# Moving sixteen subtractions to GpSimd and nine evictions to VectorE in a fused attention, MoE and MLP kernel

## The chip, the cores and the metric

The kernel runs on 1 core of one Trainium2 chip. The metric is the device time of one execution in microseconds (us). A core has a matrix engine (TensorE, PE in the profile, with its weight loads as PEld), a vector engine (VectorE, DVE), a scalar engine (ScalarE, ACT), GpSimd (POOL) and SyncE (SP), which here issues the transfers. Each engine works through its own instructions in the order in which they were issued, and waits where one needs a result that isn't there yet.

## What is computed

The reference has three stages, one after the other:

```
attn = softmax(mask(q @ k.T / 8)) @ v           # 4 batches, 8 heads, 576 positions, head size 64
x = soft mixture of experts(attn)               # 2304 tokens x 512, 8 experts of 4 slots
h = x @ w_in                                    # 2304 x 2048
g = where(h > 0, h, exp(min(h, 0)) - 1)
out = g @ w_out                                 # 2304 x 512
```

`w_in` (512 x 2048) and `w_out` (2048 x 512) arrive as 64-bit floats, the rest as 32-bit floats.

## The kernel before

The attention and the mixture of experts take the first 144 us and are issued in the order in which the code stands. The change lies in the last stage, the MLP, which is planned: the code builds a list of nodes (engine, estimated duration, what it depends on, a key that says by when it is wanted, the function that issues it), lays them out in time with a list scheduler (lines 1062 to 1102), and issues them in that order. For each engine the scheduler looks at the nodes that can start within 0.1 us of the earliest one and takes the one with the smallest key. Among the engines it takes the node that starts first. So the order on each engine is fixed before the kernel runs, from estimates, and at run time an engine can't pass over an instruction that waits.

The hidden size is cut into 16 blocks `f` of 128, the tokens into five groups (four of 512, one of 256). One unit of work is one group with one block. `SEGS` fixes the order of the units; the first ones use f = 0 and 1 for all groups. A unit is:

- `f_h` (line 974, PE): the hidden block into PSUM, from `M4` (`pers` in the trace), which is `w_in` times the mixture's 32 slot outputs;
- `f_e`, `f_r`, `f_g` (lines 978, 981 on ACT, 984 on DVE): the activation into the tile `g`. Line 984 reads PSUM and one SBUF tile;
- `f_hi` (line 990, ACT) and `f_lo` (line 994, DVE): `g` split into a rounded high part and the rest. Line 994 reads two SBUF tiles. The trace names the outputs `ghi`, `glo` or `rings`;
- `f_o` (lines 1016 to 1018, PE): for each 128 tokens three matmuls of 512 columns, high by high, high by low, low by high, added up in one of six PSUM banks (`ops`).

The weights have to be turned from 64-bit to 32-bit floats first. For each block of 128 x 512 this is line 727 (`dec_abs`) on ACT and lines 731, 735 and 741 (`dec_1` to `dec_3`) on DVE, where 735 and 741 read two SBUF tiles. For `w_out`, `out_nodes` then splits the block: line 928 on ACT writes the high part (`wh` or `w` in the trace), line 931 on DVE subtracts it from the decoded block (`wl` or `w`). This subtraction reads two SBUF tiles and runs once for each of the 16 blocks. All blocks of `w_in` pass the same decoding and then `m_nodes`, which makes `M4` with two matmuls (lines 883 and 894), two ACT instructions and line 900 on DVE.

A sum over f is done in several segments. The first segment of a token block is evicted from PSUM to SBUF (`part`) by ACT, line 1046, 18 of them; later ones are added to `part` by DVE (line 1048), the last is added and sent out (line 1051). `s` numbers the 128-token blocks in a group. An eviction's key is set by the moment at which the sixth product after it wants the same PSUM bank.

Ahead of the planned time `FT` the free time on PE is filled with matmuls whose result nobody uses (line 1111, `wps`): 0.9 of each planned gap.

Of the kernel before, what the change touches and what calls it, by code (L numbers as in the profile page):

```python
# [12 lines left out]
AF = mybir.ActivationFunctionType  # L13
# [6 lines left out]
def attn_moe_mlp(ctx, tc, q, k, v_l, v_s, phi, w1, w2, w_in, w_out, out):  # L20
    nc = tc.nc
    B, S, D = 4, q.shape[1] * q.shape[3] // 4, 64
# [32 lines left out]
    ]  # L55
    TB, SL, LD, LM, EPS = 24.7, 4.7, 2.7, -1.2, 0.1
    WP, HP = 256, 2
    K1, K2 = 0.0, 0.0
    FT, FW, M0 = 7.5, 0.9, ((0, 128), (128, 128), (256, 256))

    const = ctx.enter_context(tc.tile_pool(name="const", bufs=1))
# [290 lines left out]
    with tc.manual_schedule():  # L352
# [7 lines left out]
        for b in range(B):  # L360
            sm_ = smask[32 * b:32 * b + 32, 0, :]
            nc.gpsimd.affine_select(
                out=sm_, in_=sm_, compare_op=ALU.is_ge, fill=NEG, base=0,
# [3 lines left out]
        for e in range(2):  # L367
            nc.vector.memset(qk_t[2][1][:, e, 0:576], 0.0)
        nc.vector.tensor_copy(
            out=smask16.rearrange("p (a b) -> p a b", b=MR), in_=smask.to_broadcast([128, 16, MR])  # L370
# [14 lines left out]
        for b in range(B):  # L385
            lm = lmask[32 * b:32 * b + 32]
            nc.gpsimd.affine_select(
                out=lm[:, 0:32], in_=lm[:, 0:32], compare_op=ALU.is_ge, fill=NEG, base=0,
# [3 lines left out]
                out=lm[:, 32:64], in_=lm[:, 32:64], compare_op=ALU.is_ge, fill=NEG, base=-1,  # L392
# [29 lines left out]
        for x in (576, 1152):  # L422
            for e in range(2):
                w = x // 576 * 576
                nc.scalar.activation(
                    out=qk_t[2][1][:, e, x:x + w], in_=zero.to_broadcast([128, w]), func=AF.Copy,
                )
        for b in range(B):
            nc.scalar.activation(
                out=e0[32 * b:32 * b + 32].rearrange("p (g x) -> p g x", x=32),  # L430
                in_=ident[0:32, 0:32].unsqueeze(1).to_broadcast([32, B, 32]), func=AF.Copy,
# [146 lines left out]
        for f in emit_N(nu - 1):  # L578
# [41 lines left out]
            out=acc_sb[0], in0=acc1, scalar=wt[:, 1:2], in1=acc_sb[0], op0=ALU.mult, op1=ALU.add  # L620
# [14 lines left out]
        for x in (slice(0, 256), slice(256, 512)):  # L635
            nc.vector.scalar_tensor_tensor(
                out=acc_sb[1][:, x], in0=acc2[:, x], scalar=wt[:, 2:3], in1=acc_sb[0][:, x], op0=ALU.mult, op1=ALU.add
# [180 lines left out]
        NF = DFF // 128  # L818
# [18 lines left out]
        def node(eng, dur, deps, key, fn, alloc=None, at=0.0):  # L837
            nodes.append((eng, dur, list(deps), key, fn, alloc, at))
            return len(nodes) - 1
# [6 lines left out]
        due, need_h, need_w, now = [], {}, {}, TB  # L846
# [7 lines left out]
        d3, m_done, w_done = {}, {}, {}  # L854

        def decode_nodes(kind, i, c, key, rel, h0=0):
            at = loads.get((1 - kind, i, c), loads.get((1 - kind, i), 0.0))
            deps = [] if at else [dma[1 - kind, i]]
            k, z, h = ("ow"[kind], i, c), (512 - h0) / 512, slice(h0, 512)

            def f_abs():
                if not h0:
                    cnt["dec"] += 1
                    dec_of[k] = dec[:, cnt["dec"] % 8]
                dec_abs(w64[1 - kind, i][:, c, h], dec_of[k][:, h])

            def step(f):
                return lambda: f(w64[1 - kind, i][:, c, h], dec_of[k][:, h])

            n = node("A", 0.05 + 0.47 * z, deps, key - 3.0, f_abs, None if h0 else ("dec", rel), at)  # L870
            n = node("V", 0.065 + 0.27 * z, [n], key - 2.0, step(dec_1))
            n = node("V", 0.07 + 0.53 * z, [n], key - 1.4, step(dec_2))
            n = node("V", 0.07 + 0.53 * z, [n], key - 0.7, step(dec_3))
            d3[1 - kind, i, c, h0] = n
            return n
# [42 lines left out]
        def w_tile(d, s, f):  # L918
            if f // 8 not in d:
                d[f // 8] = slot(s, f"w{f}")  # L920
            return d[f // 8][:, 512 * (f % 8):512 * (f % 8) + 512]

        def out_nodes(f):
            key, rel = need_w[f] - 1.5 - LD, []
            x = decode_nodes(0, f // 4, f % 4, key, rel)

            def f_hi():
                nc.scalar.activation(out=w_tile(wo_hi, 0, f).bitcast(F32R), in_=dec_of["o", f // 4, f % 4], func=AF.Copy)

            def f_lo():  # L930
                nc.vector.tensor_tensor(
                    out=w_tile(wo_lo, 5, f).bitcast(F32R), in0=dec_of["o", f // 4, f % 4], in1=w_tile(wo_hi, 0, f),
                    op=ALU.subtract,
                )

            x = node("A", 0.52, [x] + ([d3[0, 1, c, 0] for c in range(4)] if f == 8 else []), key, f_hi)
            x = node("V", 0.6, [x] + ([d3[1, 1, c, 0] for c in range(4)] if f == 8 else []), key + 0.7, f_lo)
            rel.append(x)
            w_done[f] = x

# [4 lines left out]
        if WP < 512:  # L945
            key = need_h[WP // 128] - LM - 5.5
# [3 lines left out]
        for i in range(4):  # L950
            if i:
                if i == 2:
                    load_node(1, 2, wb1, [d3[1, 0, c, 0] for c in range(4)])
                if i == 3:
                    load_node(0, 3, 9, [d3[0, 2, c, 0] for c in range(4)] + [dma[1, 2]])
                    load_node(1, 3, wb1, [d3[1, 2, c, 0] for c in range(4)] + [dma[0, 3]])
                key, rels = need_h[4 * i] - LM, [[] for c in range(4)]
                m_nodes(i, 0, 512, [decode_nodes(1, i, c, key - 5.5 - 1.6 * (3 - c), rels[c]) for c in range(4)], key, rels)
            for f in range(4 * i, 4 * i + 4):
                out_nodes(f)  # L960
# [74 lines left out]
        for si, gi, s, f0, f1, y, T in ev_n:  # L1035
            k = part_n[si, gi, s]
            key = o_due[k + 6] - 1.0 if k + 6 < len(o_due) else T
            j = groups[gi][0] // 128 + s
            pt = part[j // 9][:, j % 9, :]
            deps = [y] + ([last[j]] if j in last else [])  # L1040
            ob = {}

            def f_ev(si=si, gi=gi, s=s, f0=f0, f1=f1, pt=pt, ob=ob):
                ps = ops[si, gi, s]
                if f0 == 0:
                    nc.scalar.activation(out=pt, in_=ps, func=AF.Copy)
                elif f1 < NF:
                    nc.vector.tensor_tensor(out=pt, in0=ps, in1=pt, op=ALU.add)
                else:
                    ob["t"] = p2.tile([128, DM], F32, tag="ob", name="ob")  # L1050
                    nc.vector.tensor_tensor(out=ob["t"], in0=ps, in1=pt, op=ALU.add)

            rel = []
            x = node("V" if f0 else "A", 0.6 if f0 else 0.48, deps, key, f_ev, ("ob", rel) if f1 == NF else None)
            o_rel[k].append(x)
            last[j] = x
            if f1 == NF:
                rel.append(node("S", 0.73, [x], key, lambda j=j, ob=ob: nc.sync.dma_start(
                    out=out[128 * j:128 * j + 128, :], in_=ob["t"]
                )))  # L1060

        end, order = {}, []
        free = {"P": 0.0, "A": 0.0, "V": 0.0, "S": 0.0}
        wait, after, ready = {}, {}, {e: [] for e in free}
        for n, x in enumerate(nodes):
            wait[n] = len(x[2])
# [5 lines left out]
        def start_of(n):  # L1072
            eng, dur, deps, key, fn, alloc, at = nodes[n]
            if alloc:
                size, rels = pools[alloc[0]]
                if len(rels) >= size:
                    rel = rels[len(rels) - size]
                    if not rel or any(d not in end for d in rel):
                        return 1e9
                    deps = deps + rel  # L1080
            for d in deps:
                at = max(at, end[d] + (0.0 if eng == "P" == nodes[d][0] else 0.13 if nodes[d][0] == eng else 2.0 if nodes[d][0] == "S" else 0.2))
            return max(at, free[eng])

        while len(order) < len(nodes):
            best = (1e8,)
            for e in free:
                c = [(start_of(n), nodes[n][3], n) for n in ready[e]]
                if c:
                    lim = min(c)[0] + EPS  # L1090
                    x = min((key, t, n) for t, key, n in c if t <= lim)
# [74 lines left out]
```

## Time and profile before

| | us |
|---|---|
| time, median of 3 runs | 378.37 |
| lowest and highest | 377.45, 378.55 |
| the profiled execution's own time | 376.64 |
| its span, first to last instruction | 374.9 |
| PE busy in the span | 341.6 (91%) |
| DVE busy | 255.8 (68%) |
| ACT busy | 233.9 (62%) |
| POOL busy | 35.1 (9%) |

The span leaves 1.74 us of the execution's time outside. Busy time of one engine lies beside that of the others. DVE and ACT instructions overlap their successor a little, so the start-to-start distance of two instructions is shorter than their duration. The mean granted TensorE clock over the span was 0.973. Times below are from the start of the span.

### The profile page before, as it was taken

The numbers are of one execution on the slowest core, as the hardware profiler recorded it, in microseconds if no ns is written. First come the engines' busy times: TensorE is split into PE (matmuls) and PEld (weight loads), VectorE is DVE, ScalarE is ACT, GpSimd is POOL, SyncE is SP. The second block draws the span as 40 slices with busy tenths as digits, with TensorE's granted clock in tenths as the row PEclk, the third lists the DMA queues.
The fourth block names the chain that finished last, engine by engine and source line by source line (L and its number), as shares of the span: only waits on it lengthen the run. The fifth ranks groups of instructions, "written<-read, shape, count | busy, mean of one in ns | idle before, by whom it ended". The sixth has DMA issues, their size and how long they took to land.

```text
span 374.9 us, 8089 instructions
## 1 busy us (share of the span) xinstructions
PE 341.6 (91%) x3287; PEld 249.6 (67%) x3287; DVE 255.8 (68%) x522; ACT 233.9 (62%) x462; POOL 35.1 (9%) x75
## 2 busy tenths in 40 slices
PE   6365988878799999999999999999999999999995
PEld 4344666556233337878688778888868888888884
DVE  6564858658360028979999999999854665476741
ACT  6395865325232046999999678868665666666660
POOL 8401964000020000000000000000000000000000
PEclk9598899989999999999999999999999999999999
DMA  6999999998999989764100144100000011032301
GB/s 205 394 399 392 395 331 366 379 407 319 388 412 406 408 352 379 294 226 166 59 2 0 27 200 169 55 3 0 0 2 0 0 57 57 0 114 112 113 2 57
DMA packets 23606, 71.64 MB, mean 191 GB/s; under 512 B 2192, under 2 KB 2320, under 8 KB 23568
## 3 DMA queue, kind: packets, MB, share of 16 engines
q1 hardware_dynamic: 23568, 71.12, 49.9%
q8 instruction: 26, 0.43, 0.5%
q14 instruction: 12, 0.10, 0.1%
HBM read 66.39 MB, written 4.72 MB: 190 GB/s over the span
## 4 chain that ended last, share of the span: by engine, by line
PE 83%; ACT 6%; DVE 4%; issue 3%; DMA 2%; SPq 0%; ACTq 0%
PE ops L1016 18%; PE ops L1017 17%; PE ops L1018 17%; PE hps L974 4%; PE acc L748 4%; PE s_ps L658 4%; ACT bd L258 2%; DMA kA<-in_k_dram 2%; PE xtps L334 2%; PE s_ps L200 2%; PE lo L292 2%; PE so L316 1%; PE wps L1111 1%; PE acc L574 1%; PE ptps L272 1%
## 5 line engine op out<-in xcount | busy, mean ns | idle before, releaser
L984 DVE SCALAR_TENSOR_TENSOR g<-hps,g 128x512 f32<-128x512 f32 (+1 forms) x80 | 50.6, 632 | 18.2 <-ACT g L981 18.2
L978 ACT ACTIVATE g<-hps 128x512 f32<-128x512 f32 (+1 forms) x80 | 44.2, 552 | 20.6 <-PE hps L974 19.2
L981 ACT ACTIVATE g<-g 128x512 f32<-128x512 f32 (+1 forms) x80 | 46.9, 586 | 1.4
L1018 PE MATMUL ops<-wh,glo 128*128 128x512 f32 x86 | 33.5, 390 | 0.0
L1018 PE MATMUL ops<-w,glo 128*128 128x512 f32 x86 | 33.5, 389 | 0.0
L990 ACT ACTIVATE ghi<-g 128x512 fp32r<-128x512 f32 (+1 forms) x40 | 23.5, 588 | 14.3 <-DVE g L984 12.9
L990 ACT ACTIVATE rings<-g 128x512 fp32r<-128x512 f32 (+1 forms) x40 | 23.4, 586 | 13.2 <-DVE g L984 11.1
L974 PE MATMUL hps<-pers 128*128 128x512 f32 (+1 forms) x80 | 29.3, 372 | 0.0
L1016 PE MATMUL ops<-wh,ghi 128*128 128x512 f32 x72 | 28.9, 401 | 0.0
L1016 PE MATMUL ops<-wh,rings 128*128 128x512 f32 x72 | 28.8, 400 | 0.0
L1016 PE MATMUL ops<-w,ghi 128*128 128x512 f32 x72 | 28.5, 395 | 0.0
L1017 PE MATMUL ops<-wl,ghi 128*128 128x512 f32 x72 | 28.1, 390 | 0.0
L1017 PE MATMUL ops<-w,rings 128*128 128x512 f32 x72 | 28.1, 390 | 0.0
L1016 PE MATMUL ops<-w,rings 128*128 128x512 f32 x72 | 28.1, 390 | 0.0
L1017 PE MATMUL ops<-w,ghi 128*128 128x512 f32 x72 | 28.1, 390 | 0.0
L1017 PE MATMUL ops<-wl,rings 128*128 128x512 f32 x72 | 28.0, 390 | 0.0
L523 POOL COPY v<-v 32x768 f32<-32x768 f32 (+2 forms) x28 | 20.6, 743 | 26.0 <-DMA v<-in_v_l_dram 21.9
L1018 PE MATMUL ops<-wh,rings 128*128 128x512 f32 x58 | 22.6, 390 | 0.0
L731 DVE TENSOR_SCALAR xw<-xw 128x512 int32<-128x512 int32 (+1 forms) x36 | 13.7, 389 | 13.0 <-ACT xw L727 12.9
L1018 PE MATMUL ops<-w,rings 128*128 128x512 f32 x58 | 22.6, 389 | 0.0
L225 DVE TENSOR_REDUCE mx<-s_ps 128x6 f32<-128x384 f32 (+1 forms) x20 | 10.2, 509 | 15.2 <-PE s_ps L214 9.2
L994 DVE TENSOR_TENSOR glo<-g,rings 128x512 fp32r<-128x512 f32 (+1 forms) x24 | 15.2, 632 | 7.2 <-ACT rings L990 5.0
(193 smaller groups left out, 712.3 us busy)
## 6 DMA issues: line engine op xcount, KB each, us to landing
w<-in_moe_w_dram SPq DMA_DIRECT2D x52, 512.0 KB, 9.3
w<-in_moe_w_in_dram SPq DMA_DIRECT2D x3, 2048.0 KB, 8.6
out_dram<-ob SPq DMA_DIRECT2D x18, 256.0 KB, 2.0
v<-in_v_s_dram SPq DMA_DIRECT2D x8, 512.0 KB, 8.7
xw<-in_moe_w_dram SPq DMA_DIRECT2D x8, 512.0 KB, 9.6
xw<-in_moe_w_out_dram SPq DMA_DIRECT2D x2, 2048.0 KB, 7.8
q<-in_q_dram SPq DMA_DIRECT2D x7, 576.0 KB, 9.6
kB<-in_k_dram SPq DMA_DIRECT2D x8, 288.0 KB, 8.8
```

What stands on the lines that cost most here:

```text
L523: nc.gpsimd.tensor_copy(out=o, in_=i)
L658: nc.tensor.matmul(hp[32 * g:32 * g + 32, :], siT[:, c, :], w_at(2 * a + g // 2, 0, 2 * c + g % 2), start=(c == CO[0]), stop=(c == CO[-1]),)
L748: nc.tensor.matmul(yp[32 * g:32 * g + 32, :], h1T[e][:, c, :], w_at(e, 1, c), start=(e == 0 and c < 4), stop=(e == NE - 1 and c >= 4),)
L974: nc.tensor.matmul(t["ps"], M4[:, 128 * f:128 * f + 128], cTf[:, t0:t0 + n], start=True, stop=True)
L978: nc.scalar.activation(out=t["g"], in_=t["ps"], func=AF.Exp)
L981: nc.scalar.activation(out=t["g"], in_=t["g"], func=AF.Relu, scale=-1.0, bias=1.0)
L984: nc.vector.scalar_tensor_tensor(out=t["g"], in0=t["ps"], scalar=0.0, in1=t["g"], op0=ALU.max, op1=ALU.subtract)
L990: nc.scalar.activation(out=t["hi"], in_=t["g"], func=AF.Copy)
L994: nc.vector.tensor_tensor(out=t["lo"], in0=t["g"], in1=t["hi"].bitcast(F32), op=ALU.subtract)
L1016: nc.tensor.matmul(o, t["hi"][:, c], hi, start=(f == f0), stop=False)
L1017: nc.tensor.matmul(o, t["hi"][:, c], lo, start=False, stop=False)
L1018: nc.tensor.matmul(o, t["lo"][:, c], hi, start=False, stop=(f == f1 - 1))
```

## The change

The subtraction of the high part goes from DVE to GpSimd with a planned cost of 1.4 in place of 0.6, and the keys of the whole decoding chain of `w_out` are set 0.8 earlier. Every first eviction with odd `s` goes from ACT to DVE. The planner gets a fifth engine.

```diff
-    K1, K2 = 0.0, 0.0
+    K1, K2, G0 = 0.0, 0.0, 0.8
...
-            key, rel = need_w[f] - 1.5 - LD, []
+            key, rel = need_w[f] - 1.5 - LD - G0, []
...
             def f_lo():
-                nc.vector.tensor_tensor(
+                nc.gpsimd.tensor_tensor(
...
-            x = node("V", 0.6, [x] + ([d3[1, 1, c, 0] for c in range(4)] if f == 8 else []), key + 0.7, f_lo)
+            x = node("G", 1.4, [x] + ([d3[1, 1, c, 0] for c in range(4)] if f == 8 else []), key + 0.7 - G0, f_lo)
...
+            f_on = "A" if not f0 and s % 2 == 0 else "V"
...
                 if f0 == 0:
-                    nc.scalar.activation(out=pt, in_=ps, func=AF.Copy)
+                    if s % 2 == 0:
+                        nc.scalar.activation(out=pt, in_=ps, func=AF.Copy)
+                    else:
+                        nc.vector.tensor_copy(out=pt, in_=ps)
...
-            x = node("V" if f0 else "A", 0.6 if f0 else 0.48, deps, key, f_ev, ("ob", rel) if f1 == NF else None)
+            x = node(f_on, 0.6 if f_on == "V" else 0.48, deps, key, f_ev, ("ob", rel) if f1 == NF else None)
...
-        free = {"P": 0.0, "A": 0.0, "V": 0.0, "S": 0.0}
+        free = {"P": 0.0, "A": 0.0, "V": 0.0, "S": 0.0, "G": 0.0}
```

## Rows read from the trace of the kernel before

**Rows 1.** The page: busy times, and busy tenths in forty slices of 9.4 us.
```profile
PE 341.6 (91%) x3287; PEld 249.6 (67%) x3287; DVE 255.8 (68%) x522; ACT 233.9 (62%) x462; POOL 35.1 (9%) x75
...
DVE  6564858658360028979999999999854665476741
ACT  6395865325232046999999678868665666666660
```

**Rows 2.** Busy time by stretch: PE, PEld, DVE, ACT, POOL, clock, DMA share, GB/s.
```profile
170.00:180.00 10.00, 10.00 (x46) 8.29 (x45) 10.00 (x19) 9.83 (x20) 0.00 (x0) 1.00 0.58 210
```

**Rows 3.** Timeline of PE at its first products: start us, us, instruction.
```profile
148.68 1.70 PE L1111 MATMUL wps<-ident 128*128 128x256 bf16 x14
...
150.64 0.48 PE L1016 MATMUL ops<-wh,rings 128*128 128x512 f32 x1
...
151.19 0.39 PE L1018 MATMUL ops<-wh,rings 128*128 128x512 f32 x1
```

**Rows 4.** Timeline of ACT and DVE ahead of the first products.
```profile
147.83 0.62 ACT L928 ACTIVATE wh<-xw 128x512 fp32r<-128x512 f32 x1
...
148.32 0.68 DVE L741 SCALAR_TENSOR_TENSOR xw<-xw 128x512 int32<-128x512 int32 x1
148.35 0.62 ACT L981 ACTIVATE g<-g 128x512 f32<-128x512 f32 x1
...
148.87 0.40 ACT L990 ACTIVATE rings<-g 128x256 fp32r<-128x256 f32 x1
...
148.91 0.68 DVE L931 TENSOR_TENSOR wl<-xw,wh 128x512 fp32r<-128x512 f32 x1
...
149.52 0.68 DVE L984 SCALAR_TENSOR_TENSOR g<-hps,g 128x512 f32<-128x512 f32 x1
...
150.12 0.41 DVE L994 TENSOR_TENSOR rings<-g,rings 128x256 fp32r<-128x256 f32 x1
```

**Rows 5.** ACT's evictions, and DVE's later ones: count, ns min/median/max, first and last start.
```profile
L1046 ACT ACTIVATE part<-ops x18: 572/598/613, 156.4 to 206.6; 128x512 f32<-128x512 f32 x18
...
L1048 DVE TENSOR_TENSOR part<-ops,part x20: 678/682/692, 208.4 to 295.1; 128x512 f32<-128x512 f32 x20
```

**Rows 6.** GpSimd's groups by shape: busy us, mean ns.
```profile
L523 POOL COPY v<-v 32x512 f32<-32x512 f32 x4 | 2.4, 609 | 0.2
```

**Rows 7.** GpSimd copies, DVE instructions beside them, and all instructions of those lines.
```profile
35.88 11.01 POOL L523 COPY v<-v 32x768 f32<-32x768 f32 x14 [21.89 <-DMA v<-in_v_l_dram]
...
37.93 0.67 DVE L244 TENSOR_SCALAR sm<-sm 128x16 f32<-128x16 f32 x1
...
38.92 0.61 DVE L250 TENSOR_TENSOR pst<-pst,sm 128x288 f32<-128x288 f32 x1
...
43.63 0.83 DVE L250 TENSOR_TENSOR pst<-pst,sm 128x288 f32<-128x288 f32 x1
...
L244 DVE TENSOR_SCALAR sm<-sm x20: 170/172/665, 8.8 to 89.5; 128x6 f32<-128x6 f32 x12, 128x16 f32<-128x16 f32 x8
...
L250 DVE TENSOR_TENSOR pst<-pst,sm x8: 458/460/832, 9.3 to 43.6; 128x288 f32<-128x288 f32 x8
...
L226 DVE TENSOR_TENSOR ss<-s_ps,mx x8: 457/458/458, 7.3 to 40.5; 128x288 f32<-128x288 f32 x8
```

**Rows 8.** Timeline of DVE, and PE at the fifteenth unit; idle time before in brackets.
```profile
160.70 0.69 DVE L994 TENSOR_TENSOR glo<-g,ghi 128x512 fp32r<-128x512 f32 x1 [0.31 <-ACT ghi L990]
...
185.76 0.75 DVE L900 SCALAR_TENSOR_TENSOR pers<-mp,negm,mps 128x512 fp32r<-128x512 f32 x1 [0.44 <-ACT mp L897]
...
190.16 0.69 DVE L931 TENSOR_TENSOR wl<-xw,wh 128x512 fp32r<-128x512 f32 x1 [0.31 <-ACT wh L928]
...
191.37 0.68 DVE L994 TENSOR_TENSOR rings<-g,ghi 128x512 fp32r<-128x512 f32 x1
...
193.13 0.39 PE L1018 MATMUL ops<-wh,rings 128*128 128x512 f32 x1
```

**Rows 9.** Line 1046 alone in the stretch 148 to 187 us: ACT busy, count.
```profile
148.00:187.00 39.00, 8.11 (x14) 1.00 0.52 199
```

## The prediction

> **What bounds the kernel now.** First the page's busy times: PE is busy for 341.6 of 374.9 us, and in the forty slices DVE and ACT stand at 9 together from about 150 to 200 us and ease off behind it [rows 1]. Then the busy times by stretch, because an average hides the stage: from 150 us to the end PE is at 10.00 of 10.00 at a granted clock of 1.00, the upper level of 2.4 GHz, and in the stretch shown DVE has 10.00 and ACT 9.83 too [rows 2]. PE's timeline confirms it: behind the first product at 150.64 [rows 3] its matmuls start one behind the other, and the list of PE's waits has nothing past 150 us. So the MLP costs what PE's matmuls cost, the change takes none of them away, and freeing DVE or ACT there is worth nothing by itself. Only two things can move the end: the moment of the first product, and a hole that opens in PE's row. Holes are near in the first 50 us of the stage, where DVE and ACT have almost no idle time left.
>
> **The first product.** DVE decodes the second weight block until 149.00 (148.32 + 0.68), then subtracts (148.91), then makes `g` of the second unit (149.52), then the low part of the first (150.12, done at 150.53) [rows 4]. Without the subtraction, line 984 could start when ACT's line 981 is done, at 148.97 (148.35 + 0.62), 0.55 earlier, and line 994 with it. The planner sees the same: by its own prices, gone through by hand, the low part of the first unit is planned 0.49 earlier, and so is the first product. The matmuls of line 1111 that fill the gap then get fewer by 0.9 x 0.49 / 0.107 (line 1110) = 4, of 0.12 us each (1.70 / 14 [rows 3]). On GpSimd the subtraction can start when the high part is there, at 148.45 (147.83 + 0.62 [rows 4]), or when DVE is done with the block before, at 149.00. With 1.2 us for it (below) it is done by 150.2, when a product moved by 0.45 from 150.64 [rows 3] would begin with the high parts. The gain is between 0 and 0.55; I take **-0.45**, the four matmuls less a little for the overlap in the row's 1.70.
>
> **The subtraction on GpSimd.** No row shows GpSimd with two inputs. A copy of 512 columns took 0.609 there [rows 6]; two inputs read one after the other would take twice that, 1.22. I take 1.22, with 0.61 as the lower end and the planner's 1.4 as the upper. As latency this costs nothing: it is 0.54 longer than the 0.68 on DVE [rows 4], and for the first block, one of the tightest, the old one was done at 149.59 for a product at 150.64, 1.05 of cover [rows 3, 4]. If that cover were gone, PE would wait for the difference once for each of the first blocks. The decoded block's buffer is also given back later by the same 0.54, to ACT's line 727, which runs ahead of need. GpSimd has nothing else to do in this stage, so no queue forms behind it. The Trainium skill (GPSIMD Engine Reference, Performance versus the Vector engine) has 4497 ns for a two-input add of 2048 columns, by which I estimate 1.12 for 512; no row here shows it, and with 1.12 the sum below would be about 0.25 lower.
>
> **ACT's nine evictions.** ACT loses 9 of 18 x 0.598 [rows 5]. ACT bounds nothing by itself while PE has no hole, so this is 0; it is a reserve, as ACT's late results are what DVE idles for here [rows 8].
>
> **DVE's queue.** It loses an instruction of 0.60 (start to start: 148.91 to 149.52 [rows 4]) for each block, and gains one of 0.60 for each odd eviction (line 1048, which reads PSUM too, has the same 0.68 as line 931 [rows 4, 5]). Up to the tightest product behind the start, that of the fifteenth unit, these are six subtractions (the sixth at 190.16 [rows 8]), -3.6, and seven evictions (half of 14 [rows 9]), +4.2: together **+0.6**. A late eviction would first hold the bank of the sixth product after it, and whatever is queued behind it on DVE; the planner puts it where its key allows.
>
> **What a GpSimd instruction costs DVE.** Here rows speak against the change. Beside GpSimd's back-to-back copies from 35.88 to 46.9, line 244 took 0.67 where its median is 0.17, and line 250 took 0.61 and 0.83 where its median is 0.46 [rows 7]. Line 250 reads two SBUF tiles. Line 226 reads PSUM and one SBUF tile, and none of its eight took over 0.458, with one of them in the same stretch [rows 7]. So some DVE instructions wait beside GpSimd, among them those with two SBUF inputs, and lines 735, 741 and 994 are of that kind. The three waited 0.50, 0.15 and 0.37, a mean of 0.34, behind copies of some 0.8 (11.01 / 14). Call w the wait that one subtraction puts into DVE's queue. Lower end 0 (line 244's minimum is 0.17, and a copy may meet nothing), upper end 1.22, the whole subtraction. Scaling 0.34 by 1.22 / 0.79 gives 0.53; since DVE's queue is fuller here than there, I take w = 0.6. The Trainium skill (SBUF — State Buffer, SBUF: two separate sides) states more: GpSimd and a DVE instruction with two SBUF inputs share a port pair that one holds for its whole instruction while the other is blocked. The rows above agree that there are waits (0.50 at most), and can't show whether they last the whole instruction.
>
> **The sum.** Up to the fifteenth unit DVE's queue gets 0.6 + 6 x 0.6 = 4.2 longer. Against it stand DVE's idle times there (five of them, 160.70 to 185.76 the first and the last, 2.86 together) and the time from the low part's end at 192.05 (191.37 + 0.68) to PE's use at 193.13, 1.08 [rows 8]: 3.94. What is left, 0.26, is a hole in PE's row. Behind that unit the planner's order gives PE several us of lead, and the last eight subtractions lie beside much emptier engines [rows 1]: 0. So -0.45 + 0.26 = -0.19 us. Against the profiled execution that is 376.64 - 0.19 = 376.45. That execution lies 1.73 below the median of the runs, and against the median the change gives 378.37 - 0.19 = **378.2**, no change that can be measured: 0.3% is 1.13 us, about what a measurement of this kernel can tell, so "no change" runs from 377.24 to 379.50.
>
> **Rival 1, the port: slower.** DVE gets nothing freed, because it waits for the instruction that it gave away. In rows 4 the instruction behind the subtraction is line 984 with one SBUF input; it could run for 0.60 and DVE would be held for 0.62. Where a two-input instruction comes next, DVE is held for 1.22. The mean of the two is 0.92. Then 0.6 + 6 x 0.92 = 6.1, less 3.94 of cover, is a hole of 2.2, most of it ahead of the fifteenth unit: 378.37 - 0.45 + 2.2 = **380.1**. It decides from w = (3.94 + 0.45 + 1.13 - 0.6) / 6 = 0.82 on; with w at 1.22 the time is 381.9. For it: DVE is at 10.00 of 10.00 just where blocks 2 to 5 are subtracted [rows 2, 8], its order is fixed, and the planner knows nothing of such a wait. Against it: the rows show at most 0.50, and ACT's nine lost evictions shorten the chains that DVE idles for. The page's rule, that the lock lasts the whole instruction, would make this the outcome.
>
> **Rival 2, a faster start.** The first product's high parts are there at 149.27 (148.87 + 0.40 [rows 4]) on the old order, and only the filling matmuls and the planner's wait for the low part hold PE until 150.64. If the new order lets PE begin that much earlier, 1.3 us go, with no hole behind: **377.0**. Against it: the second and third product still need the subtraction and the low part, and these move by half a microsecond at most.
>
> **How the numbers follow.** The forecast has 0.55: PE has no hole now, the terms are all under a microsecond, and they have both signs. The port has 0.37, since the rows show it at work and leave only its size open. The faster start has 0.08, as nothing behind 151 us can give time back. Faster by over 0.3%: 0.08; within: 0.55; slower: 0.37. The range begins at 377.4, the whole start gain of 0.55 and 0.4 for the spread of a median, and goes to 380.9, which is w about 1.05; past that I leave some 0.12, below 377.4 some 0.08. The forecast's own range is 377.5 to 379.3.
>
> **What would show it.** Right: PE at 10.00 in all stretches from its first product on, that product at about 150.2, line 931 on POOL at 1.2 us, and lines 735, 741 and 994 on DVE with single instructions up to 0.6 longer than 0.68. If the port decides, DVE's rows beside POOL's reach 1.3 to 1.9 us, and PE's row has holes near 160.6 (line 883, behind the late decoding), 175 to 182 and 187 to 193. The forecast is wrong if PE's row has holes of over 1.6 us together, or if the first product comes before 149.5.

## The result: 381.84 us, slower by 0.9%

| | before | after |
|---|---|---|
| median of 9 runs, us | 377.91 | 381.84 |
| lowest and highest, us | 377.0, 381.01 | 380.8, 383.35 |
| the profiled execution, us | 376.64 | 383.35 |
| its span, us | 374.9 | 381.5 |

The ratio is 1.009, with a 95% interval of 1.0061 to 1.012. The prediction had 378.2 and a range up to 380.9. Of the runs below, one of e3_order_kept (1844.96 us) and the profiled one of e2_sub_only (409.84 us, at a mean granted clock of 0.825) were disturbed: the medians count them, the ratios do not, and the trace of e2 isn't read.

**The profile after.** The page's busy times, to be read beside [rows 1]:

```profile
PE 345.5 (91%) x3283; PEld 250.9 (66%) x3283; DVE 263.3 (69%) x515; ACT 230.1 (60%) x453; POOL 61.5 (16%) x91
```

DVE gave away sixteen instructions and got nine, seven fewer, and yet is busy for 7.5 us longer. GpSimd has 26.4 us more for sixteen subtractions, 1.65 each. Busy time by stretch, with [rows 2]'s columns (PE, PEld, DVE, ACT, POOL, clock, DMA share, GB/s):

```profile
190.00:200.00 10.00, 8.73 (x38) 6.89 (x38) 10.00 (x13) 7.70 (x15) 7.17 (x4) 1.00 0.01 2
...
250.00:260.00 10.00, 9.03 (x40) 7.13 (x38) 9.92 (x13) 5.61 (x11) 4.35 (x3) 1.00 0.01 2
```

From 180 to 190 us PE has 9.59 and from 220 to 230 us 9.56. Before, PE had 10.00 in each of these four. In the two shown, which have the largest holes, DVE is full with few instructions (13 in ten us, where [rows 2] have 19) and POOL is at work. The clock is 1.00, the upper level, in all four, so it is not the clock. PE's waits from 150 us to the end, where there were none before (what waited, for what: us in total, times, longest):

```profile
PE hps L974 <- DVE g L984: 2.7, 3, 1.3
...
PE hps L974 <- DVE pers L900: 0.4, 1, 0.4
```

**Where the time went.** Two distances on PE's timeline separate the stage from what differs between two executions ahead of it: from the mixture's first matmul of line 883 to the first product (the start), and from the first product to the last (PE's row). First the kernel before, its first line 883 and its last product; the first product is in [rows 3]:

```profile
144.04 0.64 PE L883 MATMUL mps<-xw,soT 128*32 128x128 f32 x16
...
370.05 0.39 PE L1018 MATMUL ops<-w,rings 128*128 128x512 f32 x1
```

Then the changed kernel, with the first product and the largest hole:

```profile
145.90 0.64 PE L883 MATMUL mps<-xw,soT 128*32 128x128 f32 x16
...
152.00 0.48 PE L1016 MATMUL ops<-wh,rings 128*128 128x512 f32 x1
...
195.27 0.39 PE L1018 MATMUL ops<-wh,glo 128*128 128x512 f32 x1
196.93 0.50 PE L974 MATMUL hps<-pers 128*128 128x512 f32 x1 [1.27 <-DVE g L984]
...
376.67 0.39 PE L1018 MATMUL ops<-w,rings 128*128 128x512 f32 x1
```

The start went from 6.60 (150.64 - 144.04) to 6.10 (152.00 - 145.90), 0.50 gained. The row went from 219.41 to 224.67, 5.26 lost. Together 4.76, a little over the 3.9 of the medians, whose interval reaches to 4.5 (1.2% of 377.91). The span grew by 6.6; the other 1.86 lie ahead of the stage, where both kernels do the same. Matmuls of a product otherwise start 0.23 apart. The holes that stand out from this (over 0.25, and not there before) add up to 4.3: 0.57 ahead of line 974 at 181 us and as much again inside line 883's matmuls behind it, 1.43 at 195, 0.60 at 226 and 1.14 at 259; the rest is in small ones. The 0.60 is the wait for line 900, which makes a part of `M4`; at the other three in the list line 974 waits for line 984 to give its PSUM buffer back.

**What DVE did meanwhile.** DVE's timeline from the fifth to the seventh subtraction, with POOL's lines for the same time:

```profile
191.10 0.69 DVE L984 SCALAR_TENSOR_TENSOR g<-hps,g 128x512 f32<-128x512 f32 x1
191.71 1.16 DVE L741 SCALAR_TENSOR_TENSOR xw<-w,xw 128x512 int32<-128x512 int32 x1
192.79 1.78 DVE L735 SCALAR_TENSOR_TENSOR xw<-w,xw 128x512 int32<-128x512 int32 x1
194.49 1.78 DVE L994 TENSOR_TENSOR rings<-g,ghi 128x512 fp32r<-128x512 f32 x1
196.19 0.68 DVE L984 SCALAR_TENSOR_TENSOR g<-hps,g 128x512 f32<-128x512 f32 x1
```
```profile
188.76 5.26 POOL L931 TENSOR_TENSOR wl<-xw,wh 128x512 fp32r<-128x512 f32 x2 [14.38 <-ACT wh L928]
194.20 1.53 POOL L931 TENSOR_TENSOR wl<-xw,wh 128x512 fp32r<-128x512 f32 x1 [0.17 <-ACT wh L928]
```

Line 994 at 194.49 takes 1.78 in place of 0.68: GpSimd began at 194.20 and was done at 195.73, and line 994 ends 0.54 after that. All eleven lengthened DVE instructions that have two SBUF inputs and 512 columns end 0.54 to 0.55 after the subtraction beside them, and the three of line 731 with 512 columns 0.28 after. It goes the other way round too. The first of the two subtractions from 188.76 on took 3.56: DVE had instructions of lines 731, 735 and 741 back to back until line 984 at 191.10, which reads PSUM and one SBUF tile, and the subtraction was done 1.22 after that. Behind line 984 stand three DVE instructions that are 0.48, 1.11 and 1.09 too long. Line 984 at 196.19 is the one that frees the buffer for which PE's line 974 waits until 196.93. Over the stage sixteen DVE instructions, of lines 731, 735, 741 and 994 alone, are 12.4 us longer than the median of their shape, 0.77 for each of the 16 subtractions; none of the 64 instructions of line 984 with 512 columns took over 0.69.

### The profile page after: what moved, and what is told of

It is laid out like the page before. It is cut to its first block, busy times and chain, and to the rows that moved or that the text cites. A ratio compares the mean times of both kernels' runs of the same rounds, so it can differ in the third digit from the quotient of the medians.

```text
span 381.5 us, 8078 instructions
## 1 busy us (share of the span) xinstructions
PE 345.5 (91%) x3283; PEld 250.9 (66%) x3283; DVE 263.3 (69%) x515; ACT 230.1 (60%) x453; POOL 61.5 (16%) x91
## 4 chain that ended last, share of the span: by engine, by line
PE 59%; DVE 26%; ACT 6%; issue 5%; DMA 3%; ACTq 0%
PE ops L1016 11%; PE ops L1017 10%; PE ops L1018 10%; DVE xw L735 5%; DVE g L984 4%; PE acc L748 4%; DVE xw L741 4%; PE s_ps L658 4%; DMA kA<-in_k_dram 3%; DVE xw L731 3%; PE hps L974 3%; ACT bd L258 3%; DVE glo L994 3%; PE xtps L334 3%; PE s_ps L200 2%
## 5 line engine op out<-in xcount | busy, mean ns | idle before, releaser
L974 PE MATMUL hps<-pers 128*128 128x512 f32 (+1 forms) x80 | 30.1, 379 | 3.1 <-DVE g L984 2.7
L931 POOL TENSOR_TENSOR wl<-xw,wh 128x512 fp32r<-128x512 f32 x8 | 14.4, 1810 | 76.3 <-ACT wh L928 73.8
L731 DVE TENSOR_SCALAR xw<-xw 128x512 int32<-128x512 int32 (+1 forms) x36 | 17.4, 497 | 12.0 <-ACT xw L727 12.0
L994 DVE TENSOR_TENSOR glo<-g,rings 128x512 fp32r<-128x512 f32 (+1 forms) x24 | 16.1, 673 | 7.3 <-ACT rings L990 5.0
```

What stands on the lines that cost most here:

```text
L731: nc.vector.tensor_scalar(out=d, in0=d, scalar1=3, scalar2=None, op0=ALU.logical_shift_left)
L974: nc.tensor.matmul(t["ps"], M4[:, 128 * f:128 * f + 128], cTf[:, t0:t0 + n], start=True, stop=True)
L994: nc.vector.tensor_tensor(out=t["lo"], in0=t["g"], in1=t["hi"].bitcast(F32), op=ALU.subtract)
```

## The experiments

The theories: **the port** (GpSimd's subtraction holds DVE, and DVE's lateness makes holes on PE), **the load** (nine evictions more are too much for DVE), **the lateness** of GpSimd's result, and **the new order** as such. The kernel before ran anew beside each, somewhat faster than in the table above, so ratios are compared; "on the scale where before is 377.9" means the ratio times 377.91. All kernels, with start and row from their own profiles:

| kernel | median, us | before, same chip | ratio (95% interval) | start | row |
|---|---|---|---|---|---|
| before | 377.91 | | | 6.60 | 219.41 |
| the change | 381.84 | 377.91 | 1.009 (1.0061 to 1.012) | 6.10 | 224.67 |
| e1_evict_only | 378.31 | 376.78 | 1.0025 (1.0001 to 1.0049) | 6.59 | 220.75 |
| e2_sub_only | 379.51 | 376.78 | 1.0066 (1.0046 to 1.0086) | not read | not read |
| e4_unread_full | 381.97 | 376.78 | 1.0131 (1.009 to 1.0172) | 6.09 | 224.69 |
| e5_unread_short | 376.64 | 376.78 | 0.9991 (0.9966 to 1.0017) | 6.10 | 219.46 |
| e3_order_kept | 379.33 | 376.99 | 1.0047 (1.0021 to 1.0074) | 6.60 | 221.77 |
| e6_h_late | 384.81 | 376.99 | 1.0215 (1.0177 to 1.0253) | 9.21 | 224.38 |
| e7_last_eight | 377.96 | 376.99 | 1.0029 (1.0009 to 1.0049) | 6.60 | 219.95 |
| e8_first_one | 376.83 | 376.99 | 0.9999 (0.9976 to 1.0021) | 6.10 | 219.69 |
| e9_lead_after_start | 381.59 | 376.62 | 1.012 (1.0046 to 1.0193) | 6.10 | 223.03 |
| e12_sub_only_lead | 382.32 | 376.62 | 1.0134 (1.0083 to 1.0185) | 6.10 | 225.73 |
| e10_halves | 378.81 | 376.62 | 1.0053 (1.0027 to 1.0078) | 6.10 | 222.26 |
| e11_copy, one run | 376.76 | 376.62 | | 6.32 | 219.45 |

**The two halves of the change.** e1_evict_only, against the change:

```diff
-    K1, K2, G0 = 0.0, 0.0, 0.8
+    K1, K2, G0 = 0.0, 0.0, 0.0
...
-                nc.gpsimd.tensor_tensor(
+                nc.vector.tensor_tensor(
...
-            x = node("G", 1.4, [x] ...
+            x = node("V", 0.6, [x] ...
```

> Only the nine evictions go to DVE; the subtraction stays on DVE, with the old keys. If the loss comes from DVE being held by GpSimd (the port): no loss, 377.5 to 378.5 beside 377.9 before. If it comes from DVE being given nine more instructions (5.4 us) in its fullest stretch (the load): 380 to 382, all or more of the change's 381.8.

e2_sub_only, against the change:

```diff
-            f_on = "A" if not f0 and s % 2 == 0 else "V"
+            f_on = "A" if not f0 else "V"
...
-                    if s % 2 == 0:
-                        nc.scalar.activation(out=pt, in_=ps, func=AF.Copy)
-                    else:
-                        nc.vector.tensor_copy(out=pt, in_=ps)
+                    nc.scalar.activation(out=pt, in_=ps, func=AF.Copy)
```

> Only the sixteen subtractions go to GpSimd; all first evictions stay on ACT. The port: 380 to 382, with single DVE instructions lengthened by up to 1.1 us beside GpSimd's. The load: no loss, and the first product some 0.5 earlier, about 377.4.

On the scale where before is 377.9, e1 is 378.9 (1.0025 x 377.91), between the two theories' numbers, and e2 is 380.4, the port's. The evictions alone cost 0.25%, the subtractions alone 0.66%, and within the intervals the two add up to the change's 0.9%. So the larger part is the subtractions', and the load has a share while DVE also keeps the subtractions: e1's row is 1.3 longer, with one hole at 181 us where line 883 waits for DVE.

**Lateness, hold and order.** e4_unread_full, against the change:

```diff
-                    nc.tensor.matmul(o, t["hi"][:, c], lo, start=False, stop=False)
+                    nc.tensor.matmul(o, t["hi"][:, c], hi, start=False, stop=False)
```

> The changed kernel, but line 1017 multiplies by the high part in place of the low part, so that nobody on PE waits for GpSimd, which still does its sixteen subtractions in full (the output lacks the low part's product). The port: as slow as the change, 381 to 382. If the loss comes from GpSimd's result reaching PE late (1.3 to 3.6 us each): 377.4 to 378.

e5_unread_short, in addition:

```diff
-                    out=w_tile(wo_lo, 5, f).bitcast(F32R), in0=dec_of["o", f // 4, f % 4], in1=w_tile(wo_hi, 0, f),
+                    out=w_tile(wo_lo, 5, f)[:, 0:32].bitcast(F32R), in0=dec_of["o", f // 4, f % 4][:, 0:32],
+                    in1=w_tile(wo_hi, 0, f)[:, 0:32],
```

> As e4_unread_full, but each subtraction covers 32 of its 512 columns (the output lacks the low part's product). The issue order of all engines is that of the change. The port: GpSimd holds little, so the loss goes, 377.4 to 378. If the loss comes from the new order, or from the evictions in it: still 381 to 382.

This pair settles the main question. With nobody on PE waiting for GpSimd (e4) the row is 224.69, PE's list of waits is the change's, line for line, and the holes are at the same places: lateness cost nothing. (On the scale where before is 377.9 its time is 382.9, a little over the 381 to 382 expected.) With the same order, the same evictions on DVE and GpSimd holding for 32 columns only (e5), the row is 219.46, that of the kernel before, and the start keeps its 6.10. PE's list of waits from 150 us on is empty again. So neither the order nor the evictions in it cost anything; GpSimd's hold on DVE cost all 5.2 us. The short subtraction also gives the decoded block's buffer back earlier, but that can't be the reason: DVE, which would have to wait for the block that ACT puts into that buffer, has no idle time in the change from 160 to 250 us (10.00 in each ten us). Line 994 in e4, then in e5 (count, ns min/median/max):

```profile
L994 DVE TENSOR_TENSOR rings<-g,ghi x16: 415/680/1779, 159.6 to 362.6; 128x512 fp32r<-128x512 f32 x13, 128x256 fp32r<-128x256 f32 x3
```
```profile
L995 DVE TENSOR_TENSOR rings<-g,ghi x16: 415/682/695, 160.1 to 358.5; 128x512 fp32r<-128x512 f32 x13, 128x256 fp32r<-128x256 f32 x3
```

**Does DVE get anything?** e3_order_kept, against the change:

```diff
-                nc.gpsimd.tensor_tensor(
+                nc.vector.tensor_tensor(
```

> The issue order of the change on all engines, but the sixteen subtractions are carried out by DVE, at the place that the plan gave them on GpSimd. The port: GpSimd's sixteen subtractions hold DVE for some 11 us in all (measured in the profile of the change), more than the 9.6 us (16 x 0.60) that DVE needs to do them, so this is no slower than the change, 379.5 to 381.5 on the scale where before is 377.9. If moving them does free DVE, taking them back adds up to 9.6 us to its full queue: slower than the change, 383 or more.

The ratio of 1.0047 is 379.7 on that scale, in the range expected for the port, though its interval overlaps the change's a little (1.0061 to 1.0074). The row is 2.9 shorter than the change's, though DVE does sixteen instructions that its plan knows nothing of. Doing them cost less than having GpSimd do them. The 0.5 at the start are gone, as the first subtraction is back in DVE's way.

**How long is the hold?** e10_halves, against the change:

```diff
-                nc.gpsimd.tensor_tensor(
-                    out=w_tile(wo_lo, 5, f).bitcast(F32R), ...
+                for h in (slice(0, 256), slice(256, 512)):
+                    nc.gpsimd.tensor_tensor(
+                        out=w_tile(wo_lo, 5, f)[:, h].bitcast(F32R), ...
```

> The change with each subtraction on GpSimd in two instructions of 256 columns. If GpSimd holds DVE for a whole instruction and no longer: DVE's longest single wait falls from 1.1 to about 0.5 us, and the time to 379 to 381. If DVE is held as long as any of GpSimd's work is queued: waits of 1.1 and more stay, 381.5 or slower.

e11_copy, against e4_unread_full:

```diff
-                nc.gpsimd.tensor_tensor(...)
+                nc.gpsimd.tensor_copy(out=w_tile(wo_lo, 5, f).bitcast(F32R), in_=dec_of["o", f // 4, f % 4])
```

> As e4_unread_full, but GpSimd copies the decoded block in place of subtracting (one input; the low part is wrong and nobody reads it). If the hold lasts as long as the instruction, whatever it reads: DVE's waits stay and are up to the copy's own time less what DVE has running, some 0.4 us in place of 1.1. If only two inputs on GpSimd block DVE: no DVE instruction over 0.75 us beside it.

Line 735 in e10, the copy and line 994 (here 991) in e11:

```profile
L735 DVE SCALAR_TENSOR_TENSOR xw<-w,xw x23: 409/677/1265, 138.2 to 236.1; 128x512 int32<-128x512 int32 x16, 128x256 int32<-128x256 int32 x7
```
```profile
L931 POOL CAST wl<-xw x8: 613/617/1349, 147.6 to 192.4; 128x512 fp32r<-128x512 f32 x8
...
L991 DVE TENSOR_TENSOR rings<-g,ghi x16: 415/684/1101, 159.9 to 358.2; 128x512 fp32r<-128x512 f32 x13, 128x256 fp32r<-128x256 f32 x3
```

With halves the longest wait on DVE is 0.59 in place of 1.11, their sum 9.0 in place of 12.4, the row 222.26, and the time 379.9 on that scale, as expected for a hold of one instruction. The copy, 0.62 long, makes single DVE instructions up to 0.42 longer, so one input on GpSimd is enough to block; but only six DVE instructions are hit, 2.1 in all, and the row is 219.45. The copy also needs no high part and so starts at other moments. The hold goes with the length of GpSimd's instruction: at most 1.11 with 1.29, 0.59 with 0.73, 0.42 with 0.62 and 0.07 with 0.26 (the times are GpSimd's shortest or usual ones).

**Which subtractions?** e7_last_eight and e8_first_one are e2 with the condition in `out_nodes`; the node's engine, cost and key follow the same `g`:

```diff
+            g = f >= 8          # e8: f == 0
...
-                nc.gpsimd.tensor_tensor(
+                (nc.gpsimd if g else nc.vector).tensor_tensor(
...
```

Expected of e7, then of e8:

> Only the last eight subtractions (blocks 8 to 15, which lie beside emptier engines) go to GpSimd; evictions stay on ACT. By the prediction's step (these cost nothing): 377.5 to 378.2. If a wait of 1.1 us on DVE makes a hole wherever line 974 waits for line 984: 378.5 to 380, with holes between 215 and 260 us.

> Only the first block's subtraction goes to GpSimd; evictions stay on ACT. The start is 0.5 us earlier and DVE waits once, by some 0.4 us: 377.3 to 377.7 beside 377.9, a ratio of 0.998 to 1.000. If one wait is enough to make a hole in PE's row: no gain, 377.9 to 378.5.

The last eight alone cost 0.29%, which is 379.0 where before is 377.9, so they aren't free. But their row is only 0.54 longer, less than half of what they cost in the change's order, and the one wait on PE's list, 0.2 at 240 us, is a product that waits for line 1051, not line 974 for line 984, as the second alternative had it. The first one alone keeps the 0.5 at the start and loses 0.28 in the row: no difference that can be measured. It is the best that any real form of the change came to, and it doesn't beat the kernel before.

**Is it line 974's place?** e6_h_late, against the change, with e9 and e12 (on e2) limited to later uses:

```diff
                     deps = deps + rel
+                    if alloc[0] == "h":        # e9, e12: and len(rels) >= 14
+                        at = max(at, max(end[d] for d in rel) + 1.4)
```

Expected of e6, of e9 and of e12:

> The change with one more line in the planner: a node that takes one of the two PSUM buffers of line 974 is planned 1.4 us after that buffer is free. If PE's holes arise because line 974 stands in PE's order at the very moment at which the plan expects DVE's line 984 to free the buffer: the holes of 0.6 to 1.4 us get shorter or go, 377.5 to 380. If PE runs out of products because the low parts or the weights come late: no better than the change, 381 or more.

> As e6_h_late, but the 1.4 us of planned lead begin only with the fifteenth use of the two PSUM buffers, so that the start keeps the change's order. If line 974, planned at the very moment at which its buffer comes free, is where DVE's waits turn into holes: the start is 6.1 us behind the first mixture matmul as in the change, the holes shrink from 4.3 us to under 1.5, and the time is 377.5 to 379. If the holes come from products that lack their inputs: 381 or more.

> The subtractions alone on GpSimd (evictions on ACT), with the same lead as e9. If the lead covers DVE's waits: 376.5 to 377.5 beside 377.0 before, the start's 0.5 kept. If DVE's waits of up to 1.1 us reach PE in another way: 378 to 380, as without the lead.

None of them helped. By their own terms e6 and e9 came out on the second alternative (386.0 and 382.4 on that scale), and e12, at 383.0, above both of its own. Yet on PE's lists of waits a product that waits for its inputs has only 0.3 (e6), nothing (e9) and 0.7 (e12). e6 held back the third line 974 too, and PE had nothing to do for 3.9 us before the first product. e9 has the change's start and a row 1.6 shorter, and PE's wait of line 974 for line 984 is gone from the list, but a wait of line 883 for line 984 took its place, and the time can't be told from the change's. In e12 the lead also delays the matmuls that make `M4`, which use the same buffers, and one hole of 2.3 arises where line 974 waits for line 900; the clock fell behind it (last section). So a lead at one kind of instruction moves the holes; that PE stops at line 974 in the change is shown by its waits, that a better plan could avoid it is not.

## Why the prediction was wrong

- **The first product** (-0.45): right. 0.50 in the change, where PE has the four matmuls fewer (x3283 for x3287), and as much in e4, e5, e8, e9, e10 and e12, whose first subtraction is off DVE too and whose start keeps the change's order; 0.28 in e11.
- **GpSimd's 1.22 and its lateness** (nothing): the time was a little low, 1.29 at least and 1.53 to 1.61 in the median; that it costs PE nothing was right, as e4 shows.
- **The evictions' reserve and DVE's +0.6**: right as far as it went. Without the hold (e5) the row has nothing in it.
- **The wait w = 0.6**: under its measured mean, 0.77, and 0.71 over the first six subtractions. That is a size off by a fifth, and by the text's own sum it would have made a hole of 0.9. It isn't what broke the forecast: rival 1's threshold, 0.82, was not even reached, and rival 1 pays from the same cover, so its sum too would have been too small.
- **The cover of 3.94**: this is the step that failed. It added DVE's five idle times and the lead of one product, as if a wait anywhere could be paid from them. The waits came in bursts (0.48, 1.11 and 1.09 within 5 us), and PE does not stop at the product with the least lead but at line 974 in its own order, which the planner puts where it expects line 984 to have freed the buffer. Before, the lead of line 974 over that moment was only 1.1, 1.0 and 1.0 at three units in this stretch (179.9, 190.9 and 192.4 us, from the timelines of PE and DVE). The third of them before (line 984 is done at 191.46), then the same two instructions in e5, where they are lines 985 and 975:

```profile
190.77 0.69 DVE L984 SCALAR_TENSOR_TENSOR g<-hps,g 128x512 f32<-128x512 f32 x1
...
192.45 0.39 PE L974 MATMUL hps<-pers 128*128 128x512 f32 x1
```
```profile
190.99 0.68 DVE L985 SCALAR_TENSOR_TENSOR g<-hps,g 128x512 f32<-128x512 f32 x1
...
192.91 0.39 PE L975 MATMUL hps<-pers 128*128 128x512 f32 x1
```

  In e5, which has the change's order with next to no hold, the lead is 1.24. In the change the burst of 2.68 falls just ahead of this line 984, and 2.68 less 1.24 is the hole of 1.43 at 195 us but for 0.01. Up to 197 us the holes are 2.6, not 0.26.
- **"Behind that unit 0"**: failed as well. 1.7 us of holes lie at 226 and 259 us, where I read emptier engines off the slices. The reading was wrong for DVE: in [rows 1] it stands at 9 up to about 262 us, and the last eight subtractions begin from 217.7 to 262.1; only ACT was emptier. For the unit whose line 974 stands at 260.01 the lead had been 3.0 before and is 2.4 in the change's order in e5; with DVE's waits nothing was left of it.
- **Rival 1** named the cause and the kind of outcome. The rows spoke for it, and the Trainium skill (SBUF — State Buffer, SBUF: two separate sides) said that the hold lasts a whole instruction; the runs now show that, with up to 1.11 us on DVE beside a subtraction of 1.3 us, about half with halves, and an end 0.54 to 0.55 behind GpSimd's each time for 512 columns and two inputs. The other half of that rule, that the perf modes are held as well, agrees with line 731, which took 1.51 in place of 0.41 beside GpSimd, if it runs in such a mode; no run here shows that directly. I gave it 0.37 because the 0.50 in [rows 7] looked like a limit. It was the most that a wait behind copies of 0.8 us happened to show.
- **The Trainium skill's price** for two inputs (GPSIMD Engine Reference, Performance versus the Vector engine), from which I estimated 1.12, was lower than the 1.29 measured at least.

## What to carry to other kernels

Moving an elementwise instruction from VectorE to GpSimd frees VectorE only if what VectorE does meanwhile leaves GpSimd's port alone, as line 984 with its PSUM input does; otherwise it waits for the instruction that it gave away, and here that cost more (0.77 each) than the instruction (0.60 from start to start). Where the order is fixed by a plan, don't pay an unplanned wait from the sum of idle times: look at where the bound engine stands in line for the late one, and at the lead there, wait by wait. Short GpSimd instructions hold less, and one alone at the right place (the first subtraction here) can be harmless.

## What the runs showed of the hardware that I had not expected

- DVE can starve GpSimd in turn: a subtraction, 1.29 at the shortest, took 3.56 beside DVE's unbroken row of lines 731, 735 and 741, and was done 1.22 after the start of a DVE instruction with PSUM and one SBUF input. That it could only begin its work there is inferred from these times.
- In e6, after 3.93 us without a matmul, PE's matmuls started 0.43 apart in place of 0.23 from 155.0 to 157.5 us, and the granted clock of the stretch is 0.66, between the lower level of 1.2 GHz and the upper of 2.4. In e12, behind the wait of 2.18 for line 900, they started 0.43 apart from 192.7 to 195.7 us, at 0.83 for the stretch. First e6, then e12:

```profile
150.00:160.00 10.00, 7.30 (x21) 5.31 (x22) 9.41 (x22) 6.65 (x16) 1.27 (x1) 0.66 0.87 325
```
```profile
190.00:200.00 10.00, 7.79 (x26) 6.00 (x27) 9.84 (x16) 8.00 (x16) 3.44 (x3) 0.83 0.01 2
```

  Behind the change's largest wait, 1.27, the clock stayed at 1.00. So a hole on PE can cost more than its own length: in e12 the slow spacing adds some 1.6 us (eight times 0.20) to the hole of 2.3. That may be what the matmuls of line 1111 ahead of the first product are worth; no run here leaves them out.
